# Seven weight conversions instead of four ahead of the joint slots, without blank matmuls, and maxima ahead of reciprocals

## The chip, the core and the metric

The kernel runs on one core of one Trainium2 chip. The metric is the device time of one execution in microseconds (us). A core has five engines that work side by side, each through its own queue in order: TensorE (PE) multiplies and transposes, VectorE (DVE), ScalarE (ACT) and GpSimd (POOL) do elementwise work, and SyncE (SP) issues the DMA transfers.

## What is computed

Sliding-window attention with eight global keys, and behind it two layers with 2048 hidden units. All of it is in float32: the kernel splits operands into a high and a low half and sums three products of them.

```python
def _attn_ref(q, k, v, n_global, n_local):          # 2 x 8 heads x 768 x 64
    scores = scale * np.matmul(q, k.transpose(0, 1, 3, 2))
    keep = is_global | is_local
    dist = np.where(is_global & ~is_local, float(n_local), np.abs(rel).astype(np.float32))
    scores = scores + (-slopes[:, None, None] * dist[None, :, :])[None]
    scores = np.where(keep, scores, -1000000000.0)
    a = np.exp(scores - np.max(scores, axis=-1, keepdims=True))
    a = a / (np.sum(a, axis=-1, keepdims=True) + 1e-09)
    return np.matmul(a, v).astype(np.float32)

def _moe_ref(x, w_in, w_out, alpha):                # 1536 x 512, 512 x 2048, 2048 x 512
    h = x @ w_in
    return ((np.maximum(h, 0.0) + alpha * np.minimum(h, 0.0)) @ w_out).astype(np.float32)

def _moe2_ref(x, w_in, w_out, a, b):                # as above, with g = P(h) / Q(h)
    ...
```

The weights arrive as float64. A weight is turned into float32 by integer operations, which is what is called a conversion here.

## The kernel before

**Steps and slots.** Attention runs in 24 steps (u = 0 to 23), each with two pairs of heads of one block of 128 queries. The steps 0 to 9 run by themselves (`alone`, the opening). The steps 10 to 23 run together with the first layer: `joint_slot(s)`, s = 0 to 15, holds the step 10 + s, the first product of weight chunk s (`first`, 12 matmuls into bank 3) and the second product of the chunk before (`second`, 12 matmuls). From slot 16 on (`plain_slot`) there are only the layers.

**A step.** Scores (PE, L433, three products for each head), maxima (DVE, L448, which also adds the mask and the distances), exponentials and their sums (ACT, L455), sum plus a small number (POOL, L472), reciprocal (DVE, L473), normalising (POOL, L467, four instructions), transposes of the result (PE, L484 and L486) and their copies (ACT, L495), product with the values (PE, L508 and L510) and the split of the result x into halves (ACT L520, DVE L521). The inputs k and q of a later block are transposed (PE, L401) and split (ACT L408 and L411 for the high half, DVE L409 and L412 for the low half, klo and qlo). A step of the opening works on several blocks at different stages: the transposes belong to the step two before, the values to the step three before. The first blocks of k and q come through `boot`, which lies in two of the four stage buffers.

**Conversions.** A weight chunk of 128 x 512 is loaded into one of four stage buffers (SP, L269). ACT scales its upper words (L325). DVE joins them with the lower words (the joins: L314, L315, L316). Then the high half is written, by POOL in the opening (L304) and by ACT in the slots (L302), and DVE subtracts it (L305). These parts are spread over `tick`s: two in a step or slot, one on either side of the other work. A conversion that starts at one tick is joined at the next, or in the tick after when `spread` is set, gets its high half after that and its low half in the following tick. `plan_weights` holds the table of ticks: tick 2u - 20 is the first of step u, 2s the later one of slot s. Before, four conversions start at the ticks -10, -8, -6 and -5 (steps 5 to 7), and from tick 0 to 13 one starts at every tick, two in a slot; then one in a slot. The first half of the weights is also written back to memory (`spill`) and read again later (`reload`).

**Order.** There is no scheduler: each engine's queue is in the order of the code. In `alone` it is scores, sum and reciprocal and normalising of the step before (`both_ready(u - 1)`), maxima of this step (`biased(u)`), low halves of the inputs, values, transfers, exponentials with the first tick between them, transposes and copies, the next inputs, second tick. DVE meets the reciprocal ahead of the maxima there. In the joint slots (`opening`, `turning`) the order is the same.

**The start.** Nine matmuls on the identity (`WARM`), masks (`window_masks`; POOL scales them for each head, L355 and L359), and in the steps 0 and 1 four more matmuls each whose result is not read, the blank matmuls (L578). `global_keys` copies the eight global keys into each of five blocks, high and low: ten small copies on POOL (L416), in step 0 and again in step 12.

Of the kernel before, what the change touches and what calls it, by code (L numbers as in the profile page):

```python
# [8 lines left out]
F32 = mybir.dt.float32  # L9
# [8 lines left out]
P = 128  # L18
B, H, S, D = 2, 8, 768, 64
NB = S // P  # L20
# [4 lines left out]
NC = DM // P  # L25
# [4 lines left out]
NG = 8  # L30
WIN = NPREV + NG + P
KST = P + NG
# [4 lines left out]
NU = NZ // 2  # L37
JOIN = 20
KL, QL, VL, BL = 12, 10, 4, 3
WARM, KEEP = 9, 2  # L40
WL = (4, 6, 8, 10)
LATE = 16
NEARLY = 4
NST = 4
CH = NF // 2
KEPT = CH + 4
# [14 lines left out]
class Kernel:  # L61
# [67 lines left out]
    def constants(self):  # L129
# [7 lines left out]
            )  # L137
        self.boot = {}
        for i in range(2):
            t = self.stage[i].rearrange("p c f w -> p (c f w)").bitcast(F32)  # L140
            for n, nm in enumerate(("k", "q")):
                self.boot[nm, i] = t[:, n * DM : (n + 1) * DM].rearrange("p (h d) -> p h d", h=H)
        for i, heads in ((0, slice(0, H // 2)), (0, slice(H // 2, H)), (1, slice(0, H))):
# [77 lines left out]
    def plan_weights(self):  # L221
        self.steps = [(0, 0, fc, fc % NEARLY) for fc in range(CH)]
        self.steps += [(0, 1, fc, fc % NEARLY) for fc in (*range(NEARLY, CH), *range(NEARLY))]
        self.steps += [(0, 2, fc, fc) for fc in range(NF)]
        self.steps += [(0, g, fc, fc) for g in (0, 1) for fc in range(CH, NF)]
        self.steps += [(1, g, j, j) for g in (2, 0) for j in range(CH)]
        self.steps += [(1, 1, j, j) for j in range(NF)]
        self.steps += [(1, g, j, j) for g in (2, 0) for j in range(CH, NF)]
        runs = [s[:2] for s in self.steps]
        self.begins = {n for n in range(len(runs)) if n == 0 or runs[n - 1] != runs[n]}  # L230
        self.ends = {n - 1 for n in self.begins if n} | {len(runs) - 1}
        self.saves = {n for n in self.ends if runs[n] in runs[n + 1 :]}
        self.adds = {n for n in self.ends - self.saves if runs[n] in SAVED}
        jobs = {}
        for fc in range(CH):
            jobs[2 * fc - 5 if fc > 2 else 2 * fc - 10] = 0, fc, "in", fc % NEARLY
            jobs[2 * fc - 2 if fc else -5] = 0, fc, "out", fc % NEARLY
        half, layer = NGR * CH, NGR * NF
        spare = [(fc, kind) for fc in range(CH, NF) for kind in ("in", "out")]
        for t, (fc, kind) in enumerate(spare):  # L240
            jobs[11 + 2 * t if fc < KEPT else 15 + 2 * t] = 0, fc, kind, None if fc < KEPT else fc
# [6 lines left out]
        times += range(107, 160, 5)  # L248
        for t in times:
            ready = [x for x in todo if x[1] <= t]  # L250
            if ready:
                j, _, kind = job = min(ready)
                todo.remove(job)
                jobs[t] = 1, j, kind, j
        assert not todo
        self.starts = set(jobs)
        self.plan = [jobs[t] for t in sorted(jobs)]
# [67 lines left out]
            nc.scalar.mul(self.de[n % 2], self.staged(n)[:, :, :, 1].bitcast(F32), 2.0**-112)  # L325


    def window_masks(self, pool):
# [14 lines left out]
        nc.vector.tensor_scalar(glo, self.idx, ng, None, ALU.is_lt)  # L343
        nc.vector.tensor_add(dist, rel, far)
        nc.vector.tensor_copy(dist0, dist[:, own])
        nc.vector.scalar_tensor_tensor(only, dist[:, o8], FAR, glo, ALU.is_ge, ALU.mult)
        nc.vector.tensor_scalar(far[:, 0:NG], only, -1.0, 1.0, ALU.mult, ALU.add)
        nc.vector.tensor_mul(dist0[:, 0:NG], dist0[:, 0:NG], far[:, 0:NG])
# [14 lines left out]
    def attention_window(self, pool, moe):  # L363
# [47 lines left out]
            nc.scalar.mul(hi, t, -0.125)  # L411
            return lambda: nc.vector.scalar_tensor_tensor(lo, t, -0.125, hi.bitcast(F32), ALU.mult, ALU.subtract)  # L412

        def global_keys(b):
            for t in (khi, klo) if b < NB - 1 else ():
                nc.gpsimd.tensor_copy(t[:, :, b * KST + P : (b + 1) * KST], t[:, :, 0:NG].bitcast(F32))  # L416

        def width(z):
            return P if (z // 4) % NB == 0 else WIN
# [102 lines left out]
            return lambda: None  # L522

        def inputs(u):
            if u == 0:
                return [("k", 0, far), ("q", 0, far)]
            some = [("k", 1, slice(0, NC)), ("q", 1, slice(0, NC))] if u == 1 else []
# [18 lines left out]

        def keys_of_all(u):
            if u % (2 * NB) == 0 and u < NU:
                for b in range(NB - 1):
                    global_keys(b)  # L550

        transpose_in("k", 0, 4, near)
        transpose_in("q", 0, 5, near)
        bm0, bm1, first_masks, later_masks = self.window_masks(pool)
        first_masks(range(0, H))
        split_in("k", 0, 4, near)()
        split_in("q", 0, 5, near)()
        load_va(0)
        load("k", 2)
        load("q", 2)  # L560
        load_va(1)

        lows = []

        def low_halves():
            while lows:
                lows.pop(0)()

        def alone(u):
            t = 2 * u - JOIN  # L570
            scores(u)
            both_ready(u - 1)
            biased(u)
            low_halves()
            if u < 2:
                later_masks(range(4 * u, 4 * u + 4))
                for _ in range(2 * KEEP):
                    nc.tensor.matmul(banks[2][:, 0:P], ident, ident, start=True, stop=True)  # L578
            values(u - 3)
            fetches(u)  # L580
            exponentials(2 * u)
            low = store_x(u - 3)
            self.tick(False, t in self.starts, spread=True)
            exponentials(2 * u + 1)
            low()
            self.join_step(3)
            transpose_p(u - 2, 6)
            copy_p(u - 2, 6)
            for n, (nm, i, cs) in enumerate(inputs(u)):
                bank = (3, 2)[n % 2]  # L590
                transpose_in(nm, i, bank, cs)
                lows.append(split_in(nm, i, bank, cs))
                if u < 2:
                    low_halves()
            keys_of_all(u)
# [133 lines left out]
    def moe(self):  # L729
# [123 lines left out]
        def joint_slot(s, halves):  # L853
            u = JOIN // 2 + s
            opening, turning = halves or (lambda u: None, lambda u: ())
            if s >= CH + 2 and s < CH + 2 + NEARLY:
                self.reload(s - CH - 2)
            if s == LATE - 1:
                self.spill()
            opening(u)  # L860
            if s:
                self.tick(True, 2 * s - 1 in self.starts)
# [8 lines left out]
                second(s - 1)  # L871
            if s == LATE - 1:
                self.tick(True, 2 * s + 1 in self.starts)

        def plain_slot(s):
            early, late = s - 1, s - 2
# [113 lines left out]
```

## Time and profile before

| | us |
|---|---|
| median of 3 runs (652.05 to 653.6) | 652.1 |
| the profiled execution | 652.37 |
| its span, first to last instruction | 650.6 |
| PE busy | 619.0 |
| DVE busy | 535.2 |
| ACT busy | 377.4 |
| POOL busy | 126.1 |

Busy time is a sum over stages with different limits, so it is read by stretches. The granted clock is the share of its full speed (2.4 GHz) at which TensorE ran: 0.50 is its lower level of 1.2 GHz. A row of the timeline gives start, duration, engine, line, operation, output and inputs, how many instructions stand in the row, and in brackets the idle time of the engine ahead of it with what ended it. In the opening the steps begin on DVE with L448; a joint slot begins on PE with its `first`, L743.

### The profile page before, as it was taken

Reading aid. Unit: us, or ns where it says so; the run is one execution under the profiler, and the core shown is the slowest. Engines: PE = TensorE matmul, PEld = TensorE weight load, DVE = VectorE, ACT = ScalarE, POOL = GpSimd, SP = SyncE. Lnnn points to the kernel's source line nnn. Section 1 sums busy time; section 2 is a strip of 40 time slices with the busy share of each in tenths; the row PEclk is TensorE's granted clock in tenths of the full one; section 3 lists DMA queues with packets and bytes.
Section 4 is the critical chain, followed back from the end, with each engine's and each line's share of the span. In section 5 each row is a group of like instructions: output and inputs, shape, how many; then the busy total and the mean of one; then the engine's idle time right before and its main releaser. Section 6 shows DMA issues by size and latency. Waiting matters only on the chain. (4 is left out here: it accounts for less than half of the span.)

```text
span 650.6 us, 9534 instructions
## 1 busy us (share of the span) xinstructions
PE 619.0 (95%) x3250; PEld 507.8 (78%) x3250; DVE 535.2 (82%) x1015; ACT 377.4 (58%) x787; POOL 126.1 (19%) x220
## 2 busy tenths in 40 slices
PE   7877999899999999999999999999999999999995
PEld 6656777778878888888888878888788888888783
DVE  4587799987756977967979989999999977786985
ACT  2895757666644323323333367687787766766671
POOL 4553311221220000000000003222222222222221
PEclk7998999999999999999999999999999999999999
DMA  8889599978887943421612500121120000300301
GB/s 160 191 224 255 144 286 251 291 235 249 249 277 268 360 144 98 130 65 36 193 62 65 169 26 2 42 94 58 33 97 2 0 1 1 129 2 0 130 0 71
DMA packets 84858, 82.80 MB, mean 127 GB/s; under 512 B 45313, under 2 KB 61953, under 8 KB 84801
## 3 DMA queue, kind: packets, MB, share of 16 engines
q1 hardware_dynamic: 84656, 81.98, 42.1%
q8 instruction: 27, 0.44, 0.3%
q14 instruction: 31, 0.25, 0.1%
q10 hardware_dynamic: 144, 0.13, 0.1%
HBM read 60.21 MB, written 19.92 MB: 123 GB/s over the span
## 5 line engine op out<-in xcount | busy, mean ns | idle before, releaser
L794 POOL TENSOR_TENSOR glo<-act,ghi 128x512 fp32r<-128x512 f32 (+1 forms) x49 | 65.7, 1341 | 385.4 <-ACT ghi L790 372.6
L751 ACT CAST ghi<-bank 128x512 fp32r<-128x512 f32 x48 | 28.2, 588 | 110.6 <-DVE bank L750 93.0
L743 PE MATMUL bank<-xhi,winhi_f 128*128 128x512 f32 x256 | 68.4, 389 | 0.0
L743 PE MATMUL bank<-xhi,winlo_f 128*128 128x512 f32 x256 | 68.4, 389 | 0.0
L743 PE MATMUL bank<-xlo,winhi_f 128*128 128x512 f32 x256 | 68.4, 389 | 0.0
L455 ACT ACTIVATE prob<-prob,stat 128x232 f32<-128x232 f32 (+1 forms) x96 | 44.7, 469 | 26.2 <-DVE stat L448 24.5
L467 POOL TENSOR_SCALAR prob<-prob,rec 128x232 f32<-128x232 f32 (+1 forms) x96 | 41.4, 450 | 93.3 <-DVE rec L473 73.3
L743 PEld LDWEIGHTS bank<-xhi,winlo_f 128*128 128x128 f32 x256 | 48.1, 188 | 10.0
L743 PEld LDWEIGHTS bank<-xhi,winhi_f 128*128 128x128 f32 x256 | 48.0, 188 | 10.0
L743 PEld LDWEIGHTS bank<-xlo,winhi_f 128*128 128x128 f32 x256 | 48.0, 188 | 10.0
L315 DVE SCALAR_TENSOR_TENSOR dx<-de,dx 128x512 int32<-128x512 int32 x64 | 48.2, 754 | 2.2
L752 DVE TENSOR_TENSOR glo<-bank,ghi 128x512 fp32r<-128x512 f32 x48 | 33.1, 689 | 16.8 <-ACT ghi L751 9.4
L790 ACT CAST ghi<-act 128x512 fp32r<-128x512 f32 (+1 forms) x49 | 30.2, 616 | 28.3 <-DVE act L787 28.2
L316 DVE SCALAR_TENSOR_TENSOR dx<-stage,dx 128x512 int32<-128x512 int32 x64 | 44.3, 692 | 2.2
L761 ACT ACTIVATE stage<-bank 128x512 f32<-128x512 f32 (+1 forms) x49 | 28.8, 588 | 29.6 <-PE bank L743 29.6
L749 DVE TENSOR_SCALAR act<-bank,al 128x512 f32<-128x512 f32 x48 | 35.8, 745 | 12.1 <-PE bank L743 12.1
L770 DVE SCALAR_TENSOR_TENSOR stage<-stage,abs_b 128x512 f32<-128x512 f32 (+1 forms) x49 | 36.0, 737 | 11.6 <-ACT stage L762 11.5
L325 ACT ACTIVATE de<-stage 128x512 f32<-128x512 f32 x64 | 42.8, 674 | 0.6 <-DMA stage<-in_moe_w_out_dram 0.6
L809 PE MATMUL bank<-wouthi_f,glo 128*128 128x512 f32 x144 | 41.3, 391 | 0.7 <-POOL glo L794 0.7
L809 PE MATMUL bank<-wouthi_f,ghi 128*128 128x512 f32 x144 | 41.1, 390 | 0.2 <-ACT ghi L790 0.2
L809 PE MATMUL bank<-woutlo_f,ghi 128*128 128x512 f32 x144 | 40.9, 389 | 0.0
L785 DVE SCALAR_TENSOR_TENSOR stage<-stage,cq,bank 128x512 f32<-128x512 f32 (+1 forms) x49 | 35.9, 734 | 3.7 <-ACT bank L775 3.7
(206 smaller groups left out, 1448.8 us busy)
## 6 DMA issues: line engine op xcount, KB each, us to landing
stage<-in_moe_w_in_dram SPq DMA_DIRECT2D x32, 512.0 KB, 4.2
stage<-in_moe_w_out_dram SPq DMA_DIRECT2D x32, 512.0 KB, 4.2
part<-saved_f SPq DMA_DIRECT2D x16, 256.0 KB, 4.3
va<-in_v_dram SPq DMA_DIRECT2D x13, 256.0 KB, 6.2
saved_f<-part SPq DMA_DIRECT2D x12, 256.0 KB, 2.6
out_dram<-part SPq DMA_DIRECT2D x11, 256.0 KB
rawk<-in_k_dram SPq DMA_DIRECT2D x10, 256.0 KB, 5.1
rawq<-in_q_dram SPq DMA_DIRECT2D x10, 256.0 KB
```

The lines of the kernel that those rows point to most:

```text
L315: lambda: nc.vector.scalar_tensor_tensor(y, e, -(2**31), y, ALU.bitwise_and, ALU.bitwise_or),
L316: lambda: nc.vector.scalar_tensor_tensor(y, low, 29, y, ALU.logical_shift_right, ALU.bitwise_or),
L325: nc.scalar.mul(self.de[n % 2], self.staged(n)[:, :, :, 1].bitcast(F32), 2.0**-112)
L455: nc.scalar.activation(p[:, j - e, :w], p[:, j - e, :w], AF.Exp, bias=st[:, j : j + 1], scale=-1.0, accum_out=st[:, 4 + j : 5 + j],)
L467: nc.gpsimd.tensor_scalar(p[:, j, :w], p[:, j, :w], r[:, e + j : e + j + 1], 1.0, ALU.mult, ALU.mult)
L743: nc.tensor.matmul(bk, w["in", a][:, c, :], x[:, c, :], start=e == 0, stop=e == len(seq) - 1)
L749: nc.vector.tensor_scalar(t, h, 0.0, self.al[:, fc : fc + 1], ALU.min, ALU.mult)
L752: return lambda: nc.vector.tensor_sub(lo, h, hi.bitcast(F32))
L770: nc.vector.scalar_tensor_tensor(w, w, self.ab[:, 0:1], ab, ALU.add, ALU.mult)
L785: nc.vector.scalar_tensor_tensor(w, w, self.cq[:, 0:1], r, ALU.add, ALU.mult)
L794: nc.gpsimd.tensor_tensor(lo, u, hi.bitcast(F32), ALU.subtract)
L809: nc.tensor.matmul(y[d], lhs, rhs, start=begin and e == 0, stop=last and e == 2)
```

## The change

It has six parts. (1) In the table of ticks seven conversions start in the opening, at -14, -12, -10, -8, -6, -4 and -2, one in each of the steps 3 to 9; the others start at 0, 2, 3, 5, 6, 8, 9, 11, 12, 13, 14 and then one in a slot, so that to tick 14 there are four in three slots. The loads begin one step earlier (`WL`), and `boot` lies in the stage buffers 2 and 3. (2) The blank matmuls of the steps 0 and 1 are gone. (3) In `alone` the maxima stand ahead of `both_ready`. (4) The far half of the first k and q is transposed and split at the very start, the second block in step 0, each into a bank of its own, and the low halves of the near half go between the masks' instructions. (5) The key copies are two instructions for all five blocks, and stand behind the low halves. (6) Small moves: the constants of the layers one step later, the last spill behind a tick, and the last five conversions of the second layer at 121, 125, 137, 141 and 145 in place of 122, 127, 132, 137 and 142.

```diff
-WARM, KEEP = 9, 2
-WL = (4, 6, 8, 10)
+WARM = 9
+WL = (2, 4, 6, 8)
...
-            t = self.stage[i].rearrange("p c f w -> p (c f w)").bitcast(F32)
+            t = self.stage[NST - 2 + i].rearrange("p c f w -> p (c f w)").bitcast(F32)
...
-        for fc in range(CH):
-            jobs[2 * fc - 5 if fc > 2 else 2 * fc - 10] = 0, fc, "in", fc % NEARLY
-            jobs[2 * fc - 2 if fc else -5] = 0, fc, "out", fc % NEARLY
+        begin = {"in": (-14, -12, -8, -4, 0, 3, 6, 9), "out": (-10, -6, -2, 2, 5, 8, 11, 13)}
...
-        def global_keys(b):
-            for t in (khi, klo) if b < NB - 1 else ():
-                nc.gpsimd.tensor_copy(t[:, :, b * KST + P : (b + 1) * KST], t[:, :, 0:NG].bitcast(F32))
+        def global_keys():
+            for t in (khi, klo):
+                blocks = t.rearrange("p c (b k) -> p c b k", k=KST)[:, :, 0 : NB - 1, P:]
+                first = t[:, :, 0:NG].bitcast(F32).unsqueeze(2).broadcast_to([P, NC, NB - 1, NG])
+                nc.gpsimd.tensor_copy(blocks, first)
...
         transpose_in("k", 0, 4, near)
         transpose_in("q", 0, 5, near)
-        bm0, bm1, first_masks, later_masks = self.window_masks(pool)
+        transpose_in("k", 0, 3, far)
+        transpose_in("q", 0, 2, far)
+        firsts = [split_in("k", 0, 4, near), split_in("q", 0, 5, near)]
+        lows = [split_in("k", 0, 3, far), split_in("q", 0, 2, far)]
...
+        bm0, bm1, first_masks, later_masks = self.window_masks(pool, near_lows)
...
             scores(u)
+            biased(u)
             both_ready(u - 1)
-            biased(u)
             low_halves()
+            keys_of_all(u)
             if u < 2:
                 later_masks(range(4 * u, 4 * u + 4))
-                for _ in range(2 * KEEP):
-                    nc.tensor.matmul(banks[2][:, 0:P], ident, ident, start=True, stop=True)
...
-                bank = (3, 2)[n % 2]
+                bank = 3 if u else 6 + n
...
-            if u == 1:
+            if u == 2:
                 self.moe_constants()
```

**Three places in the order of instructions.** Names: bank is a PSUM bank, stage a stage buffer, dx a joined weight, winlo and woutlo a low half of a weight, rec the reciprocals, prob the scores and probabilities, stat their maxima and sums. The maxima are printed as ISA.

DVE, a whole step of the opening with a conversion, before (the first conversion, in step 6):

```order
L448 ISA prob_255,stat_260<-bank_87,bm_285 128x232
L448 ISA stat_260 128x1
L409 TENSOR_TENSOR klo<-bank_85,khi 128x4x128
L314 TENSOR_SCALAR dx_96<-de_94 128x512
L315 SCALAR_TENSOR_TENSOR dx_96<-de_94,dx_96 128x512
L316 SCALAR_TENSOR_TENSOR dx_96<-stage_90,dx_96 128x512
L521 TENSOR_TENSOR xlo_108<-bank_84,xhi_105 128x2x128
L305 TENSOR_TENSOR winlo__112<-dx_96,winhi__111 128x512
L473 RECIPROCAL rec_263<-rec_263 128x4
L448 ISA prob_256,stat_261<-bank_82,bm_285 128x232
```

and after, in step 5:

```order
L453 ISA prob_259,stat_262<-bank_87,bm_293 128x232
L453 ISA stat_262 128x1
L478 RECIPROCAL rec_263<-rec_263 128x4
L414 SCALAR_TENSOR_TENSOR qlo_253<-bank_85,qhi_251 128x512
L315 TENSOR_SCALAR dx_97<-de_95 128x512
L316 SCALAR_TENSOR_TENSOR dx_97<-de_95,dx_97 128x512
L317 SCALAR_TENSOR_TENSOR dx_97<-stage_91,dx_97 128x512
L526 TENSOR_TENSOR xlo_108<-bank_84,xhi_105 128x2x128
L306 TENSOR_TENSOR winlo__116<-dx_97,winhi__115 128x512
L453 ISA prob_254,stat_260<-bank_82,bm_293 128x232
```

The reciprocal, for which POOL's normalising waits, moved from ahead of the four maxima to behind them, next to the joins.

PE, the end of the scores of step 0 and what follows, before:

```order
L433 MATMUL bank_87<-khi,qlo_252 128x128
L578 MATMUL bank_84<-part_78 128x128 x4
L401 MATMUL bank_85<-part_78,stage_90 128x128 x2
L401 MATMUL bank_84<-part_78,stage_90 128x128 x2
L433 MATMUL bank_82<-khi,qhi_250 128x128
```

and after:

```order
L438 MATMUL bank_86<-khi,qlo_252 128x128
L438 MATMUL bank_87<-khi,qlo_252 128x128
L403 MATMUL bank_88<-part_78,stage_93 128x128 x4
L403 MATMUL bank_89<-part_78,stage_93 128x128 x4
L438 MATMUL bank_82<-khi,qhi_250 128x128
```

The four blank matmuls and the far half of the first block stood there; now it is the second block, in two other banks.

DVE in the joint slot 5, from the low half of x to the low half of the layer's input, before:

```order
L521 TENSOR_TENSOR xlo_109<-bank_84,xhi_106 128x2x128
L305 TENSOR_TENSOR woutlo__118<-dx_96,wouthi__117 128x512
L314 TENSOR_SCALAR dx_98<-de_94 128x512
L315 SCALAR_TENSOR_TENSOR dx_98<-de_94,dx_98 128x512
L316 SCALAR_TENSOR_TENSOR dx_98<-stage_92,dx_98 128x512
L305 TENSOR_TENSOR winlo__124<-dx_97,winhi__123 128x512
L314 TENSOR_SCALAR dx_96<-de_95 128x512
L315 SCALAR_TENSOR_TENSOR dx_96<-de_95,dx_96 128x512
L316 SCALAR_TENSOR_TENSOR dx_96<-stage_93,dx_96 128x512
L749 TENSOR_SCALAR act_99<-bank_85,al 128x512
L750 SCALAR_TENSOR_TENSOR bank_85<-bank_85,act_99 128x512
L412 SCALAR_TENSOR_TENSOR qlo_253<-bank_84,qhi_251 128x512
```

and after:

```order
L526 TENSOR_TENSOR xlo_109<-bank_84,xhi_106 128x2x128
L306 TENSOR_TENSOR woutlo__118<-dx_96,wouthi__117 128x512
L306 TENSOR_TENSOR winlo__124<-dx_97,winhi__123 128x512
L315 TENSOR_SCALAR dx_98<-de_94 128x512
L316 SCALAR_TENSOR_TENSOR dx_98<-de_94,dx_98 128x512
L317 SCALAR_TENSOR_TENSOR dx_98<-stage_92,dx_98 128x512
L752 TENSOR_SCALAR act_99<-bank_85,al 128x512
L753 SCALAR_TENSOR_TENSOR bank_85<-bank_85,act_99 128x512
L414 SCALAR_TENSOR_TENSOR qlo_253<-bank_84,qhi_251 128x512
```

One set of three joins left the slot.

## Rows read from the trace of the kernel before

**Rows 1.** Stages: stretch in us, length, busy time by engine, clock, DMA

```profile
9.10:19.30 10.20, 9.29 (x50) 8.51 (x50) 3.58 (x22) 4.57 (x19) 8.02 (x31) 0.50 1.06 189
19.30:56.90 37.60, 27.29 (x286) 21.09 (x284) 29.77 (x105) 30.44 (x99) 19.28 (x47) 1.00 0.91 232
56.90:60.30 3.40, 3.40 (x30) 2.93 (x28) 2.21 (x12) 2.70 (x9) 1.95 (x5) 0.50 1.13 351
60.30:140.00 79.70, 73.56 (x525) 59.79 (x524) 68.59 (x172) 52.56 (x142) 17.73 (x51) 1.00 0.81 237
```

**Rows 2.** Waits of PE (total, times, longest): 70 to 130, 130 to 141, 400 to 500

```profile
PE bank L508 <- DVE qlo L412: 2.5, 3, 1.5
PE bank L508 <- DVE klo L409: 2.0, 2, 1.0
...
PE bank L508 <- DVE klo L409: 0.8, 1, 0.8
...
PE bank L809 <- POOL glo L794: 0.7, 1, 0.7
```

**Rows 3.** Timeline of PE, first matmuls of the slots 0, 4, 5, 9, 10

```profile
60.66 1.21 PE L743 MATMUL bank<-xhi,winhi__111 128*128 128x512 f32 x4 [0.20 <-DVE klo L409]
...
96.74 1.19 PE L743 MATMUL bank<-xhi,winhi__111 128*128 128x512 f32 x4
...
106.50 1.20 PE L743 MATMUL bank<-xhi,winhi__115 128*128 128x512 f32 x4
...
144.94 1.20 PE L743 MATMUL bank<-xhi,winhi__115 128*128 128x512 f32 x4
...
153.84 1.20 PE L743 MATMUL bank<-xhi,winhi__119 128*128 128x512 f32 x4
```

**Rows 4.** Timeline of DVE, the first joins of two conversions in one slot

```profile
99.44 0.42 DVE L314 TENSOR_SCALAR dx<-de 128x512 int32<-128x512 int32 x1
...
101.83 0.42 DVE L314 TENSOR_SCALAR dx<-de 128x512 int32<-128x512 int32 x1
```

**Rows 5.** Timeline of DVE in the opening: steps 4, 6, 7 and 10

```profile
28.34 0.40 DVE L448 CUSTOM_DVE_ANT_0 prob<-bank,bm 128x232 f32<-128x232 f32 x1
...
35.98 0.40 DVE L448 CUSTOM_DVE_ANT_0 prob<-bank,bm 128x232 f32<-128x232 f32 x1
...
37.86 0.42 DVE L314 TENSOR_SCALAR dx<-de 128x512 int32<-128x512 int32 x1
...
39.65 0.42 DVE L521 TENSOR_TENSOR xlo<-bank,xhi 128x256 fp32r<-128x256 f32 x1
...
41.34 0.37 DVE L448 CUSTOM_DVE_ANT_0 prob<-bank,bm 128x232 f32<-128x232 f32 x1
...
58.63 0.40 DVE L448 CUSTOM_DVE_ANT_0 prob<-bank,bm 128x232 f32<-128x232 f32 x1 [0.96 <-PE bank L433]
```

**Rows 6.** Timeline of the steps 0 and 1: blank matmuls, first reciprocal

```profile
10.91 2.07 PE L578 MATMUL bank<-part 128*128 128x128 f32 x8
...
15.82 2.07 PE L578 MATMUL bank<-part 128*128 128x128 f32 x8
...
16.06 0.18 DVE L473 RECIPROCAL rec<-rec 128x4 f32<-128x4 f32 x1 [1.34 <-POOL rec L472]
```

**Rows 7.** Timeline of POOL and DVE, operations of both at one time

```profile
41.60 1.76 POOL L467 TENSOR_SCALAR prob<-prob,rec 128x232 f32<-128x232 f32 x4 [0.38 <-DVE rec L473]
...
43.20 0.44 DVE L314 TENSOR_SCALAR dx<-de 128x512 int32<-128x512 int32 x1
...
406.24 1.36 POOL L794 TENSOR_TENSOR glo<-act,ghi 128x512 fp32r<-128x512 f32 x1 [3.18 <-issue]
...
406.49 1.67 DVE L315 SCALAR_TENSOR_TENSOR dx<-de,dx 128x512 int32<-128x512 int32 x1
```

**Rows 8.** Timeline of PE, the transposes ahead of the scores of step 10

```profile
56.37 0.67 PE L401 MATMUL bank<-part,rawk 128*128 128x128 f32 x4 [3.35 <-DVE qlo L412]
```

**Rows 9.** Timeline of SP, the transfer of four constants

```profile
16.96 2.81 SPq L186 DMA_DIRECT2D co<-in_moe_a_dram  x1
```

More of the change, by code (lines that the diff above doesn't have):

```diff
@@ L234, in plan_weights @@
         jobs = {}
-        for fc in range(CH):
-            jobs[2 * fc - 5 if fc > 2 else 2 * fc - 10] = 0, fc, "in", fc % NEARLY
-            jobs[2 * fc - 2 if fc else -5] = 0, fc, "out", fc % NEARLY
+        begin = {"in": (-14, -12, -8, -4, 0, 3, 6, 9), "out": (-10, -6, -2, 2, 5, 8, 11, 13)}
+        for kind, times in begin.items():
+            for fc, t in enumerate(times):
+                jobs[t] = 0, fc, kind, fc % NEARLY
         half, layer = NGR * CH, NGR * NF
@@ L240, in plan_weights @@
         for t, (fc, kind) in enumerate(spare):
-            jobs[11 + 2 * t if fc < KEPT else 15 + 2 * t] = 0, fc, kind, None if fc < KEPT else fc
+            jobs[12 + 2 * t if fc < KEPT else 15 + 2 * t] = 0, fc, kind, None if fc < KEPT else fc
         todo = []
@@ L247, in plan_weights @@
         times = [t for t in range(48, 96) if (t % 2 == 0 or t in (55, 71) or t > 82) and t not in (64, 66, 80, 82, 85, 88, 91, 94, 95)]
-        times += range(107, 160, 5)
+        times += (107, 112, 117, 121, 125, *range(137, 160, 4))
         for t in times:
@@ L325, in tick, with window_masks @@
             nc.scalar.mul(self.de[n % 2], self.staged(n)[:, :, :, 1].bitcast(F32), 2.0**-112)
-    def window_masks(self, pool):
+    def window_masks(self, pool, between):
         nc, rel = self.nc, self.rel
@@ L345, in window_masks @@
         nc.vector.tensor_copy(dist0, dist[:, own])
+        between()
         nc.vector.scalar_tensor_tensor(only, dist[:, o8], FAR, glo, ALU.is_ge, ALU.mult)
@@ L524, in inputs @@
         def inputs(u):
-            if u == 0:
-                return [("k", 0, far), ("q", 0, far)]
-            some = [("k", 1, slice(0, NC)), ("q", 1, slice(0, NC))] if u == 1 else []
+            some = [("k", 1, slice(0, NC)), ("q", 1, slice(0, NC))] if u == 0 else []
             i, odd = divmod(u + 3, 2)
@@ L548, in keys_of_all, with near_lows @@
             if u % (2 * NB) == 0 and u < NU:
-                for b in range(NB - 1):
-                    global_keys(b)
+                global_keys()
         transpose_in("k", 0, 4, near)
         transpose_in("q", 0, 5, near)
-        bm0, bm1, first_masks, later_masks = self.window_masks(pool)
+        transpose_in("k", 0, 3, far)
+        transpose_in("q", 0, 2, far)
+        firsts = [split_in("k", 0, 4, near), split_in("q", 0, 5, near)]
+        lows = [split_in("k", 0, 3, far), split_in("q", 0, 2, far)]
+        def near_lows():
+            for low in firsts:
+                low()
+        bm0, bm1, first_masks, later_masks = self.window_masks(pool, near_lows)
         first_masks(range(0, H))
-        split_in("k", 0, 4, near)()
-        split_in("q", 0, 5, near)()
         load_va(0)
@@ L561, in attention_window @@
         load_va(1)
-        lows = []
         def low_halves():
@@ L589, in alone @@
             for n, (nm, i, cs) in enumerate(inputs(u)):
-                bank = (3, 2)[n % 2]
+                bank = 3 if u else 6 + n
                 transpose_in(nm, i, bank, cs)
                 lows.append(split_in(nm, i, bank, cs))
-                if u < 2:
-                    low_halves()
-            keys_of_all(u)
             self.tick(False, t + 1 in self.starts, spread=u < JOIN // 2 - 1)
-            if u == 1:
+            if u == 2:
                 self.moe_constants()
@@ L857, in joint_slot @@
                 self.reload(s - CH - 2)
-            if s == LATE - 1:
-                self.spill()
             opening(u)
@@ L873, in joint_slot @@
                 self.tick(True, 2 * s + 1 in self.starts)
+                self.spill()
         def plain_slot(s):
```

## The prediction

> **What bounds the kernel now.** I read three views in this order: the stages with granted clock, then what TensorE (PE) waits for, then the two engines that it waits for. The stages [rows 1] show three different limits. From 60 to 140 us, the joint slots, PE is busy 73.6 of 79.7 us and VectorE (DVE) 68.6, and the granted clock is 1.00. Every wait of PE in that stretch ends with DVE writing a low half, qlo or klo [rows 2]: 2.5 + 2.0 + 0.8 = 5.3 us. From 19 to 57 us, the later opening, nothing is packed: PE is busy 27.3 of 37.6 us, DVE 29.8, ScalarE (ACT) 30.4. Before 19 us and again from 56.9 to 60.3 us the clock stood at 0.50, its 1.2 GHz level. After 140 us PE hardly waits; the one late wait that this change can touch is 0.7 us [rows 2].
>
> So a conversion in a joint slot is dear only where DVE has no room. The first pass of slot 4 began at 96.74 and that of slot 5 at 106.50 [rows 3]: 9.76 us with two conversions, of which PE waited 1 to 1.5. Slots 9 to 10, with one conversion, took 8.90 (144.94 to 153.84), with no wait: that is PE's own work. One conversion costs DVE 101.83 - 99.44 = 2.39 us [rows 4]. So DVE needs about 9.76 us with two, 7.4 with one, and 8.2 on average at four in three slots.
>
> **Part by part. The joint slots, -5.2.** Three conversions leave these slots. DVE's average of 8.2 lies under PE's 8.9. A slot that still has two runs 0.86 over, one with one leaves 1.5, and before the change PE's first wait of about 1 us came only after three full slots in a row. The change has two such slots in a row at most (6 and 7). I take back 5.2 of the 5.3 us; the ends are 4.0 and 5.6.
>
> **The first steps, -4.3 up to step 4.** Two groups of blank matmuls go, 2.07 us each [rows 6], both ahead of transposes that the next scores need: at most 4.1. DVE waited 1.34 us for the sums of POOL at step 1 [rows 6], behind ten small key copies that become two: at most 1.3 more. Against it stand the transposes of the far half, now ahead of the first scores, and low halves ahead of the masks, together some tenths. The maxima no longer wait for the reciprocals, but the mask rows on POOL then become the last to arrive. The ends are -3.7 and -5.2; I take -4.3, so the maxima of step 4 begin at 24.0 in place of 28.34 [rows 5].
>
> **Steps 4 to 9, +6.0.** Before, from the maxima of step 4 to those of step 10 it is 58.63 - 28.34 = 30.3 us [rows 5]. Only step 6 on had joins. Such a step took 41.34 - 35.98 = 5.36 us [rows 5]: four maxima, low half of the input, three joins from 37.86, x's low half at 39.65, then a short wait for POOL's high half and the low half of the weight. DVE works in all of it but that wait, so it sets the length. Now each of the steps 4 to 9 has a conversion, and step 9 the joins of a second one (39.65 - 37.86 = 1.8).
>
> The length of a step changes too. The reciprocal now stands behind the maxima, so POOL's four normalisings (1.76 us [rows 7]) start 1.3 us later and run beside the three joins in place of beside the maxima. The trace shows what two such operations do to each other: the join of 406.49 took 1.67 us in place of 0.69, because a POOL subtraction ran from 406.24 to 407.60 [rows 7]; the join waited it out. A normalising is short and lets go early: the join of 43.20 began while the last of the four was running and took 0.44 in place of 0.42 [rows 7]. With a hold of about 0.3 us for each, three of them fall between the joins: the second join waits about 0.15 us, the third 0.1, and POOL's high half comes some 0.15 later. I take 5.75 us a step. The ends are 5.36 (no meeting) and 6.65 (single file: maxima 1.3, 0.35 until POOL starts, 1.76, 1.8, and some 1.45 for the two halves, of the 1.69 from 39.65 to 41.34). The Trainium skill, SBUF — State Buffer, section "Who interferes with whom", says that VectorE and GpSimd share a port pair as an exclusive lock, held for the whole instruction, when VectorE has two SBUF inputs or a two-port mode; that is the third rival below, and row 406.49 agrees with it.
>
> So step 10 begins at 24.0 + 5 x 5.75 + 5.75 + 1.8 = 60.3 in place of 58.63. The two parts together give -4.3 + 6.0 = **+1.7**.
>
> **The hand-over, +2.3.** The first pass of the joint slots waits for bank 3, which DVE frees 2.0 us after the maxima of step 10 begin (58.63 to 60.66 [rows 3, 5]). Before, PE idled 3.35 us at 53 to 56.4 [rows 8], then ran 3.4 us at clock 0.50 [rows 1]: work that lay ahead of the slots, half of it hidden by DVE. Now DVE's double step 9 leaves PE idle for some 4.5 us right ahead of the first pass, so the low clock falls on dense slots. One stretch of 3.4 us at half speed costs 1.7, two cost 3.4, none 0; I take 2.3. The Trainium skill, TensorE: Matmul & The Clock Gate, section "What's actually happening", has the throttled state as the default, released by activity, and so speaks against taking blank matmuls out. The trace bears it out only in part: with the blanks in place the clock was 0.50 for 10.2 us [rows 1].
>
> **The rest.** The last weights are converted at other ticks, two of them one or two ticks earlier and three later, away from the end of a group near 470 us, where PE waited 0.7 us for POOL's low half: -0.5, between 0 and -0.7. The constants' three transfers move one step later and now stand ahead of the second weight load on SP; the issue of one of them held SP for 2.81 us [rows 9], so ACT may wait as long for that load in step 4. DVE's longer steps 4 and 5 cover it; without that cover it costs up to 2.8. The weights use other stage buffers than the first keys and queries, so no load waits for them. The last spill moves behind a tick and delays the reloads by some 3 us; they are read 20 us later. The keys' copies in slot 2 shrink beside idle time of POOL: nothing.
>
> **Sum.** -5.2 + 1.7 + 2.3 - 0.5 = -1.7. The profiled execution took 652.37 us (650.6 of span and 1.8 around it), which gives 650.7; the median of the runs, 652.1, lies 0.3 lower. I forecast **650.4**: within 0.3% of before, which is about what a measurement of this kernel can tell from no change (650.1 to 654.1).
>
> **The rivals.**
> *Joins and normalisings do not hurt each other, and the clock holds.* For it: the 0.44 of row 43.20. Step 10 then begins at 24.0 + 5 x 5.36 + 7.16 = 58.0, which is -0.7; with the clock at half its price, +1.2, the sum is -0.7 + 1.2 - 5.2 - 0.5 = -5.2, or **647.0**.
> *A step of the opening runs in single file.* At 6.65 us a step, six steps cost 5.4 more than I took: **655.8**, slower than before. It decides from about 6.4 us a step. For it: row 406.49, where a join waited a whole POOL operation. Against it: row 43.20.
> *The joint gain does not come.* If slots with two conversions still make PE wait, 5 us less are won: **655**. Against it: slots 8 to 10 with one conversion show no wait.
> *It does not do what it says:* seven conversions do begin before the slots by the order of instructions, so I give this nothing.
>
> **How the numbers follow.** Forecast, 650 to 654: 0.44. First rival, below 650.1: 0.40. Single file: 0.12. No joint gain: 0.04. Faster 0.40, within 0.44, slower 0.16. For eight in ten the range leaves out the far ends of the first and the second rival: 646.8 to 654.8. Both signs stay in it; the forecast's own range is 649 to 653.
>
> **What would show it.** Right: no wait of PE on qlo or klo over 0.5 us from 60 to 140 us; maxima of step 4 at 23 to 25 us; steps 4 to 8 of 5.6 to 6.0 us on DVE, with joins over 0.75 us; the first pass at 61.5 to 63 us, at clock 0.50. Wrong: steps of 5.4 or 6.5 us, a first pass before 60 us, or joint slots still over 9.3 us.

## The result, and the profile after

The changed kernel took 657.16 us, median of four runs (655.97 to 657.87), against 652.09 for the kernel before beside it: a ratio of 1.0069, interval 1.0054 to 1.0083. It is slower, and the time lies outside the forecast range. The profiled execution took 655.97 with a span of 654.1 (before: 652.37 and 650.6). It is the shortest of its four runs, so the traces can explain 3.5 of the 5.1 us between the medians; where the other 1.6 arise, no trace here shows. A ratio, here and below, compares the runs of both kernels and need not be the quotient of their medians. Differences between two variants are differences of their medians, whose runs spread by 0.3 to 3 us; one of about 1 us says little by itself, and the marks of the traces carry the readings.

Seven marks of the two timelines show where it went. Each is the start of a row: the first maximum of a step on DVE, or the first matmul of a slot's `first` on PE.

| mark | before | after | difference |
|---|---|---|---|
| maxima of step 4 | 28.34 | 24.38 | -3.96 |
| maxima of step 10 | 58.63 | 66.33 | +7.70 |
| first pass of slot 0 | 60.66 | 68.32 | +7.66 |
| first pass of slot 1 | 69.49 | 79.61 | +10.12 |
| first pass of slot 16 | 200.91 | 205.74 | +4.83 |
| last first pass | 628.45 | 634.42 | +5.97 |
| end of the span | 650.6 | 654.1 | +3.5 |

So the first steps gain 4, steps 4 to 9 lose 11.7, slot 0 loses 2.5, the joint slots gain 5.3, the stretch to the last first pass loses 1.1, and the tail is 2.5 shorter.

The large term is in one step. DVE's timeline (start, duration, engine, line, operation; in brackets the idle time ahead and what ended it) has the maxima of steps 4, 5, 6 and 10, and between two of them one join:

```profile
24.38 0.40 DVE L453 CUSTOM_DVE_ANT_0 prob<-bank,bm 128x232 f32<-128x232 f32 x1 [0.80 <-PE bank L438]
...
30.03 0.39 DVE L453 CUSTOM_DVE_ANT_0 prob<-bank,bm 128x232 f32<-128x232 f32 x1
...
39.85 0.69 DVE L317 SCALAR_TENSOR_TENSOR dx<-stage,dx 128x512 int32<-128x512 int32 x1 [5.20 <-DMA stage<-in_moe_w_in_dram]
...
41.89 0.39 DVE L453 CUSTOM_DVE_ANT_0 prob<-bank,bm 128x232 f32<-128x232 f32 x1
...
66.33 0.37 DVE L453 CUSTOM_DVE_ANT_0 prob<-bank,bm 128x232 f32<-128x232 f32 x1
```

Step 4 takes 5.65 us, step 5 takes 11.86, and steps 6 to 8 take 5.64 each. In step 5 the third join of a weight waits 5.2 us for a weight load. Yet ScalarE had scaled that same weight at 29.55, so its load had landed by then. The ScalarE row and, from SP's timeline, the load that it waited for and a later one:

```profile
29.55 0.67 ACT L326 ACTIVATE de<-stage 128x512 f32<-128x512 f32 x1 [2.69 <-DMA stage<-in_moe_w_in_dram]
...
25.26 0.43 SPq L270 DMA_DIRECT2D stage<-in_moe_w_in_dram  x1
...
33.48 0.38 SPq L270 DMA_DIRECT2D stage<-in_moe_w_in_dram  x1
```

The join waited for the load issued at 33.48, 6.4 us earlier, and not for the one at 25.26. The stages (columns as in [rows 1]) show the stall, the hand-over at low clock, and the joint slots, where PE no longer waits:

```profile
30.00:42.00 12.00, 6.04 (x50) 5.32 (x52) 5.29 (x17) 6.75 (x21) 3.24 (x7) 0.76 1.11 308
...
60.00:68.30 8.30, 3.44 (x32) 2.71 (x32) 7.55 (x23) 5.08 (x17) 5.79 (x10) 0.71 0.97 290
68.30:79.60 11.30, 10.86 (x76) 8.86 (x76) 4.37 (x14) 5.76 (x16) 1.35 (x5) 0.76 0.55 152
79.60:140.00 60.40, 60.34 (x426) 49.30 (x424) 52.26 (x131) 39.00 (x109) 13.18 (x35) 1.00 0.75 211
```

### The profile page after: what moved, and what is told of

Same layout as the page of the kernel before. It is cut to its first block, busy times and chain, and to the rows that moved or that the text cites. A ratio compares the mean times of both kernels' runs of the same rounds, so it can differ in the third digit from the quotient of the medians.

```text
span 654.1 us, 9467 instructions
## 1 busy us (share of the span) xinstructions
PE 623.7 (95%) x3234; PEld 510.6 (78%) x3234; DVE 538.4 (82%) x1015; ACT 376.2 (58%) x785; POOL 133.6 (20%) x206
## 4 chain that ended last, share of the span: by engine, by line
PE 79%; DVE 10%; POOL 4%; ACT 3%; issue 2%; DMA 1%; SPq 0%; DVEq 0%; POOLq 0%; ACTq 0%
PE bank L812 36%; PE bank L746 36%; POOL prob L472 2%; PE bank L513 2%; PE bank L438 2%; DVE prob L453 1%; DVE dx L316 1%; PE bank L489 1%; DMA dwinhi_f<-spare 1%; PE bank L515 1%; DVE act L790 1%; PE bank L491 1%; DVE stage L789 1%; PE bank L403 1%; DVE stage L788 1%
## 5 line engine op out<-in xcount | busy, mean ns | idle before, releaser
L797 POOL TENSOR_TENSOR glo<-act,ghi 128x512 fp32r<-128x512 f32 (+1 forms) x49 | 67.2, 1371 | 385.3 <-ACT ghi L793 364.0
L472 POOL TENSOR_SCALAR prob<-prob,rec 128x232 f32<-128x232 f32 (+1 forms) x96 | 46.7, 504 | 95.6 <-DVE rec L478 60.1
L316 DVE SCALAR_TENSOR_TENSOR dx<-de,dx 128x512 int32<-128x512 int32 x64 | 50.9, 795 | 2.2
L317 DVE SCALAR_TENSOR_TENSOR dx<-stage,dx 128x512 int32<-128x512 int32 x64 | 45.9, 718 | 7.3 <-DMA stage<-in_moe_w_in_dram 5.2
```

What stands on the lines that cost most here:

```text
L316: lambda: nc.vector.scalar_tensor_tensor(y, e, -(2**31), y, ALU.bitwise_and, ALU.bitwise_or),
L317: lambda: nc.vector.scalar_tensor_tensor(y, low, 29, y, ALU.logical_shift_right, ALU.bitwise_or),
L472: nc.gpsimd.tensor_scalar(p[:, j, :w], p[:, j, :w], r[:, e + j : e + j + 1], 1.0, ALU.mult, ALU.mult)
L797: nc.gpsimd.tensor_tensor(lo, u, hi.bitcast(F32), ALU.subtract)
```

## Which load the join waits for

The table `WL` issues one weight load at the end of each of the steps 1 to 4 (2, 4, 6, 8 are twice the step; loads and weights are counted from 0 here). The first conversion now begins in step 3, and its joins run in step 4, ahead of the table's last entry. Behind the joins stands `load_more`, which refills the ring of four stages: it issues loads 3 and 4. Then the table's fourth entry calls `load_next`, which takes whatever comes next: load 5, into the stage of weight 1, whose low words DVE has not read yet. The order of SP's instructions shows this load with what it waits for, first in the changed kernel, then with the table stopped at four loads (`waits` names the queues and engines that it waits for):

```
L270 DMA stage_91<-in_moe_w_in_dram 128x4x256 [waits DMAHW2_49,Activation_49]
...
L270 DMA stage_91<-in_moe_w_in_dram 128x4x256 [waits DMAHW3_49,DVE_49,Activation_49]
```

In the changed kernel it waits for ScalarE's scaling but not for DVE's join; the join, later in program order, waits for the load. It also takes the last three bits of the numbers of the second `w_in` chunk from the fourth chunk, which load 5 brings, so this is a change of what is computed as well. (The expectation below calls it another matrix; it is another chunk of the same one.) Before, `WL` began one step later, but the first joins only came in step 6, when all four loads had been issued.

**Four loads only.**

```diff
-            if 2 * u in WL:
+            if 2 * u in WL and self.loads < NST:
```

> The changed kernel with one condition added: the opening's own table of weight loads stops once four loads have been issued. Theory A: in the changed kernel the first conversion's joins now come in step 4, ahead of the table's fourth entry; the join's own refill then issues loads 3 and 4, and the table's entry issues load 5 into the stage that still holds weight 1, so that the third join of step 5 has to wait for load 5 (5.2 us at 39.85) and takes its low words from that other matrix. With the condition, step 5 has no wait for a load over 0.7 us and lasts 5.65 us like its neighbours, the maxima of step 10 begin near 60.1 in place of 66.33, and the time falls by 6.2 from 657.2 to 651.0 (649.5 to 652). Rival C: the wait is for a late load behind the constants' transfers; then the condition changes nothing and the time stays at 656 to 658.

Measured: 650.84 (ratio to before 0.9956, 0.9933 to 0.9979). Theory A holds. The wait for a load is gone; step 5 lasts 7.17 in place of 11.86, step 10 begins at 62.32. Load 5 now goes out when the join that reads its stage is done:

```profile
35.30 0.69 DVE L317 SCALAR_TENSOR_TENSOR dx<-stage,dx 128x512 int32<-128x512 int32 x1
...
36.05 0.37 SPq L270 DMA_DIRECT2D stage<-in_moe_w_in_dram  x1
```

The medians are 6.3 us apart, the spans of the two traces 4.4. Step 5 does not last the 5.65 that I expected: 1.5 us are left, of which below.

**Constants out of the way, the overrun left in.**

```diff
-            if u == 2:
+            if u == 5:
                 self.moe_constants()
```

> The changed kernel with the three transfers of the constants issued at the end of step 5 in place of step 2, so that they no longer stand ahead of the second weight load. Theory A (a load into a stage that is still read): the wait of the third join in step 5 stays at 4 to 6 us and the time at 656 to 658; the wait of 2.69 us of ScalarE for the second load in step 4 shrinks below 1 us and gives nothing back. Rival C (the constants make the second load late, and that is what the join waits for): the wait of the join goes and the time falls by about 5, to 652.

Measured: 654.02 (1.0012, 0.9997 to 1.0028). The join still waits for a load, as A says:

```profile
38.09 0.69 DVE L317 SCALAR_TENSOR_TENSOR dx<-stage,dx 128x512 int32<-128x512 int32 x1 [4.22 <-DMA stage<-in_moe_w_in_dram]
```

ScalarE's wait of 2.69 is gone. But the time fell by 3.1 where I expected no change. The traces show 1.8 of it: load 5 lands earlier too (join at 38.09 in place of 39.85, step 10 at 64.56 in place of 66.33). C names a second, smaller cost and not the cause of the stall.

## The constants ahead of the second weight load

With four loads only, ScalarE waits 2.96 us in step 4 for the second load; the forecast took this as covered by DVE. DVE loses nothing by it in step 4, but in step 5 it waits 0.91 for ScalarE's high half and 0.46 for the scores, with PE at clock 0.53, and the step lasts 7.17. The wait of ScalarE, the two waits of DVE, and the stage of step 5:

```profile
30.14 0.68 ACT L326 ACTIVATE de<-stage 128x512 f32<-128x512 f32 x1 [2.96 <-DMA stage<-in_moe_w_in_dram]
...
33.23 0.69 DVE L414 SCALAR_TENSOR_TENSOR qlo<-bank,qhi 128x512 fp32r<-128x512 f32 x1 [0.91 <-ACT qhi L413]
...
37.88 0.40 DVE L453 CUSTOM_DVE_ANT_0 prob<-bank,bm 128x232 f32<-128x232 f32 x1 [0.46 <-PE bank L438]
...
30.70:37.90 7.20, 5.62 (x39) 4.96 (x40) 5.29 (x17) 6.77 (x21) 3.27 (x7) 0.53 1.13 294
```

ScalarE, with its wait behind it, is busy for 6.77 of these 7.2 us.

> The changed kernel with four opening loads only, and the constants' three transfers at the end of step 5 in place of step 2. Against four opening loads alone (650.84). Theory: with the constants ahead of it the second weight load reached ScalarE 2.96 us late in step 4, the chain behind that made step 5 last 7.17 in place of 5.64, so that term of the prediction was not covered; now ScalarE waits under 0.5 us for that load, step 5 lasts 5.6 to 5.8, and the time falls by 1.5 to about 649.3. Rival (step 5 was long only because the clock stood at 0.53 there): the step stays above 6.8 us and the time does not change.

The edit is that of the constants above, on top of the four loads. Measured: 651.76 (0.998, 0.9969 to 0.9991), no gain. Step 5 did fall to 5.64, but step 7 rose to 6.75: the constants' first reader on ScalarE, left at the end of step 6, now waited for them, and behind it POOL's sums and DVE's reciprocal.

```profile
44.78 0.20 ACT L192 ACTIVATE abs_b<-co 128x2 f32<-128x2 f32 x1 [3.36 <-DMA co<-in_moe_b_dram]
...
44.67 0.18 DVE L478 RECIPROCAL rec<-rec 128x4 f32<-128x4 f32 x1 [1.02 <-POOL rec L477]
```

So I moved the readers too.

```diff
-            if u == 2:
+            if u == 5:
                 self.moe_constants()
-            if u == 6:
+            if u == 9:
                 self.moe_constants_ready()
```

> The changed kernel with four opening loads only, the constants' transfers at the end of step 5 and their first readers at the end of step 9 in place of step 6. In the run before, with the readers left at step 6, ScalarE waited 3.4 us for the constants there and step 7 lasted 6.75. Against four opening loads alone (650.84). Theory: both waits of ScalarE are gone, all steps from 4 to 8 last 5.6 to 5.7, step 10 begins at 60.7 to 61.1 in place of 62.3, and the time falls by 1.3 to 1.6, to about 649.4. Rival (the long step 5 was the clock's doing, which differs between runs): the time stays at 650.5 to 651.8.

Measured: 650.85 (0.9964, 0.9952 to 0.9977). All steps from 4 to 8 last 5.65 and step 10 begins at 60.99, 1.33 earlier than with four loads alone, as the theory says. But the median did not move. In the traces the first pass of slot 0 comes 1.33 earlier, slot 0 takes 11.37 in place of 10.64, at a lower clock, and at the end of the span 0.4 is left, less than the runs of one kernel differ. The stage of slot 0 in both, first with four loads only, then with the constants moved:

```profile
64.30:75.00 10.70, 10.27 (x77) 8.48 (x77) 4.37 (x14) 5.81 (x16) 1.39 (x5) 0.81 0.59 170
```

```profile
63.00:74.40 11.40, 10.98 (x77) 8.97 (x77) 4.34 (x14) 5.78 (x16) 1.37 (x5) 0.76 0.72 221
```

The late load is thus a real 1.5 us in step 5. The low clock of that step went with it (1.00 in step 5 once the constants had moved), but it seems the smaller part: with blanks ahead of slot 0 (below) ScalarE's wait was 2.99, the clock of step 5 0.76 in place of 0.53, and the step still lasted 7.02. Whether the 1.5 reaches the end depends, as far as these traces go, on the hand-over behind it. The last pair below has it again.

## Maxima ahead of reciprocals

On top of the four loads, `both_ready(u - 1)` again stands ahead of `biased(u)`.

> The changed kernel with the condition on the loads, and with the reciprocals ahead of the maxima again in the opening. Theory: the joins no longer run beside POOL's normalisings, so the joins of 0.83 us return to 0.69 and steps 6 to 9 last 5.36 in place of 5.64; the first steps lose some 1 to 1.5 because the maxima wait for the sums again. Against the kernel with the condition alone: -1.7 + 1.2 = -0.5 (-1.7 to +1). Rival: the length of a step is set by something else, the joins are no cause; then steps stay at 5.6 and the time rises by 1 or more.

Measured: 650.13 (0.9944, 0.9922 to 0.9967). Both halves of the theory show: step 4 begins at 26.71 in place of 25.07, and every step from 4 to 8 lasts 5.36 in place of 5.64, step 5 in place of 7.17. That step gains 1.5 more than its neighbours because step 4 begins later, so that ScalarE waits only 0.89 for the second load. Of the 1.8 us by which step 10 begins earlier (60.50), the order itself thus gives only 0.3. Joins and normalisings of one step, with maxima first (four loads only):

```profile
45.15 2.79 POOL L472 TENSOR_SCALAR prob<-prob,rec 128x232 f32<-128x232 f32 x4 [1.49 <-DVE rec L478]
...
45.92 0.83 DVE L316 SCALAR_TENSOR_TENSOR dx<-de,dx 128x512 int32<-128x512 int32 x1
46.78 0.83 DVE L317 SCALAR_TENSOR_TENSOR dx<-stage,dx 128x512 int32<-128x512 int32 x1
48.56 0.69 DVE L306 TENSOR_TENSOR winlo__120<-dx,winhi__119 128x512 fp32r<-128x512 f32 x1 [0.61 <-POOL winhi__119 L305]
```

and with reciprocals first:

```profile
43.06 1.76 POOL L472 TENSOR_SCALAR prob<-prob,rec 128x232 f32<-128x232 f32 x4 [0.38 <-DVE rec L478]
...
45.13 0.69 DVE L316 SCALAR_TENSOR_TENSOR dx<-de,dx 128x512 int32<-128x512 int32 x1
45.86 0.69 DVE L317 SCALAR_TENSOR_TENSOR dx<-stage,dx 128x512 int32<-128x512 int32 x1
47.29 0.69 DVE L306 TENSOR_TENSOR winlo__120<-dx,winhi__119 128x512 fp32r<-128x512 f32 x1 [0.41 <-POOL winhi__119 L305]
```

Two joins lengthen by 0.14 each, the four normalisings from 1.76 to 2.79. The Trainium skill, SBUF — State Buffer, section "Who interferes with whom", has a VectorE instruction with two SBUF inputs contend with a GpSimd instruction that reads SBUF. The trace agrees that they contend; but a join lost only 0.14 us, no whole normalising of 0.44.

**The same part alone, on the kernel before.** In the kernel before, the two lines in `alone` change places.

> The kernel before with one part of the change alone: maxima ahead of reciprocals in the opening. Theory (joins beside POOL's normalisings cost 0.28 us a step): the four steps with joins last 5.64 in place of 5.36, +1.1; the first steps no longer wait for POOL's sums, up to -1.3; together between -0.2 and +1.0. Of the end of the program: in the trace of the kernel before 7.2 us lie between the last store's issue and the end, in all changed kernels 4.65 to 5.0. If that belongs to the one execution profiled, the end here is 4.6 to 5.0 too; if it belongs to the kernel before, it is 7.

Measured: 651.11 (0.9987, 0.9975 to 0.9999), 1.7 under the median of before (652.78) where I expected -0.2 to +1.0; the ten runs lie between 650.67 and 653.37, and the interval all but touches 1. The first steps gained more than I thought, 2.58 by step 4, and step 10 began 2.82 earlier. The join steps were uneven: 6.16, 5.64 and a double one of 7.01 (before 5.36, 5.37, 7.67). Of 2.85 us at slot 0, 1.6 were given back at once, since slot 0 took 10.42 in place of 8.83, part of it at low clock:

```profile
57.80:68.30 10.50, 10.07 (x77) 8.35 (x77) 4.50 (x14) 5.46 (x15) 1.40 (x5) 0.83 0.37 85
```

From the last store's issue to the end it was 6.7 us, nearer to the 7.2 of before than to the 4.65 to 5.1 of the changed kernels. So the shorter tail, 2.5 us of the sum, goes with the changed kernel. It lies wholly behind the last stores: from the last first pass to the last store's issue on SP it is 14.6 us before and after. Why the end is shorter, no run here shows.

## The blank matmuls of steps 0 and 1

The edit puts the four blank matmuls behind `later_masks` in each of the steps 0 and 1 back, on top of the four loads.

> The changed kernel with the condition on the loads, and with the blank matmuls of steps 0 and 1 put back. Theory of the prediction: each of the two groups delays the scores behind it by up to 2.07 us, so the maxima of step 4 begin 2 to 4 us after 24.4 and the time rises by 2 to 4 against the kernel with the condition alone. Rival (the blanks pay by holding up the clock): the granted clock is 1.00 for longer before 50 us, the steps that PE sets get shorter, and the time falls by up to 1.5 or stays.

Measured: 652.39 (0.9989, 0.9974 to 1.0005), 1.5 over four loads alone, less than the 2 to 4 that I expected. Step 4 began at 27.52, 2.45 later, as expected; but step 5 then lasted 5.64, since ScalarE waited only 0.65 for the second load, and step 10 began 0.94 later. The clock was no better: 0.50 from 9 to 21 us with the blanks in place, and 0.77 at the hand-over (63 to 76 us). Taking the blanks out was right.

## The late ticks

```diff
-        times += (107, 112, 117, 121, 125, *range(137, 160, 4))
+        times += range(107, 160, 5)
```

> The changed kernel with four opening loads only, and with the last eleven conversions at the ticks of the kernel before (107, 112, 117 and so on by fives). Against four opening loads alone (650.84). Theory: the new ticks cost, the difference to the kernel before grows by 0.8 us between 455 and 485 us of the trace and by 0.3 near 522; with the old ticks both go and the time falls by 1.1 to about 649.8. Rival of the prediction (the new ticks gain 0.5): the time rises by 0.5 to 651.3.

Measured: 649.77 (0.9958, 0.9944 to 0.9973), 1.07 under four loads alone: the new ticks cost what the traces showed. From the first pass of slot 16 to the last first pass it is 428.64 with four loads only and 427.54 with the old ticks, as before the change (427.54). With the old ticks PE's waits after 210 us are again those of before, 1.2 for ScalarE and 0.7 for POOL, in place of 2.3 for ScalarE; these rows make up 0.4 of the 1.1. One of the two new stalls in PE's timeline (four loads only):

```profile
465.33 1.21 PE L812 MATMUL bank<-wouthi_f,ghi 128*128 128x512 f32 x4 [0.58 <-ACT ghi L793]
```

ScalarE's high half came late because it had waited 1.19 us for DVE, which is the engine that the conversions load.

## The hand-over

**The second joins of step 9 left for slot 0.**

```diff
-            self.tick(False, t + 1 in self.starts, spread=u < JOIN // 2 - 1)
+            self.tick(False, t + 1 in self.starts, spread=True)
```

> The changed kernel with four opening loads only, and with the second conversion's joins of step 9 left for the first joint slot, where VectorE waits 4.63 us for the first pass. Against four opening loads alone (650.84). Theory: the maxima of step 10 and the first pass of slot 0 come 1.8 us earlier (60.5 and 62.5), nothing waits for the joins, and the time falls by 1.8 to about 649.0. Rival: VectorE is then late with the low halves in slot 0 or 1 and the 1.8 us come back there, so that the time stays at 650 to 651.

Measured: 648.82 (0.9941, 0.9924 to 0.9957). Slot 0 began 1.81 earlier (62.50), took 8.81 in place of 10.64 at clock 1.00, and no matmul waited for the joins. The median fell by 2.0, close to the theory's 1.8; the profiled execution is the shortest of the four (647.16, the others 648.8), and its trace gains 3.6 by slot 1.

**Blank matmuls where PE is idle.**

```diff
             if s:
                 self.tick(True, 2 * s - 1 in self.starts)
+            for _ in range(0 if s else 16):
+                nc.tensor.matmul(banks[7][:, 0:P], self.ident, self.ident, start=True, stop=True)
             first(s)
```

> The changed kernel with four opening loads only, and with 16 blank matmuls ahead of the first pass of slot 0, where TensorE waits 3.84 us for klo. Against four opening loads alone (650.84). Theory of the prediction (idle time ahead of the first pass brings the low clock onto it): the granted clock stays at 1.00 through slot 0, from the first pass of slot 0 to that of slot 1 it takes 8.9 us in place of 10.64, and the time falls by 1.7 to about 649.1. Rival: the clock falls all the same, the blanks run at 0.50 and reach past the end of the wait, and the time rises by up to 3.

Measured: 648.9 (0.9943, 0.9926 to 0.996). That is 1.9 under four loads alone. The blanks filled the wait, and slot 0, from 63.53 to 72.32, took 8.79. PE's timeline:

```profile
59.62 3.84 PE L865 MATMUL bank<-part 128*128 128x128 f32 x32
63.53 1.20 PE L746 MATMUL bank<-xhi,winhi__111 128*128 128x512 f32 x4
```

Its stage row has the clock at 1.00:

```profile
63.50:72.30 8.80, 8.35 (x76) 7.08 (x76) 4.39 (x14) 5.75 (x16) 1.36 (x5) 1.00 0.90 267
```

Compare the clock of 0.81 without them. The mechanism of the hand-over term, idle PE ahead of dense slots, is shown.

## A version that beats both

Four loads only, the old late ticks, the joins of step 9 in slot 0, and reciprocals first from step 4 on (maxima first in steps 0 to 3):

```diff
+            if u < 4:
+                biased(u)
             both_ready(u - 1)
+            if u >= 4:
+                biased(u)
```

> The changed kernel with four opening loads only, the late ticks of the kernel before, the second joins of step 9 left for slot 0, and reciprocals ahead of the maxima from step 4 on (maxima first in steps 0 to 3). If the parts add up: 650.84 - 1.1 (late ticks) - 2.0 (joins in slot 0) - 1.5 (steps of 5.36 in place of 5.64 from step 4 on) = 646.2 (645.5 to 647.5). If the gains of the opening overlap: 647.5 to 649.

Measured: 646.73 (0.991, 0.9893 to 0.9926). Step 4 lasted 5.94, the others 5.37 or 5.38. With the constants and their readers moved as well:

> The same combination, with the constants' transfers at the end of step 5 and their readers at the end of step 9. If ScalarE's wait for the second weight load was what made step 5 long: 1.5 less than the combination without this, 644.7 (644 to 646). If the clock was: no difference.

Measured: 644.68 (0.9876, 0.9859 to 0.9892), 8 us under the kernel before. The steps last 5.35 to 5.37, step 10 begins at 57.66, and in this execution the clock stands at 1.00 in all stages up to the tail:

```profile
19.00:57.60 38.60, 28.68 (x292) 22.82 (x292) 31.62 (x103) 31.30 (x97) 21.79 (x48) 1.00 0.99 253
57.60:59.60 2.00, 0.03 (x1) 0.00 (x0) 2.00 (x11) 1.47 (x6) 1.69 (x4) 1.00 0.99 367
59.60:68.50 8.90, 8.43 (x77) 7.10 (x77) 6.12 (x17) 5.93 (x16) 1.70 (x5) 1.00 1.06 289
```

Of the 2.2 between the two spans, 0.77 lie ahead of slot 0 and 1.56 in slot 0, which ran partly at low clock without the constants moved (10.39 against 8.83); the rest differs by 0.1 the other way. This compares one trace of each. Two of the four runs with the constants moved, 645.26 and 645.54, had a mean clock of 0.98 in place of 1.00, so that moving the constants settles the clock of slot 0 is not shown.

## Why the prediction was wrong

**The step that failed** is in the part "The rest", where loads were costed at nothing: "The weights use other stage buffers than the first keys and queries, so no load waits for them". That looked at who had the stages before, and not at the two places that issue loads. `WL` moved by one step and the first joins by two, so the refill overtook the table. Its price was 11.86 - 7.17 = 4.7 us in step 5. The order of the instructions shows it without any time: on SP the sixth weight load does not wait for DVE's join that reads the same stage.

**A second sentence of that part failed too**: "DVE's longer steps 4 and 5 cover it; without that cover it costs up to 2.8". The cover held in step 4 and not in step 5; the cost was 1.5, inside its own bound. I took DVE as the only engine that sets a step; ScalarE's delay came to DVE by way of its high half (0.91) and of the scores (0.46).

**The late ticks** were given -0.5 and cost 1.1: the wait for POOL [rows 2] went, and two for ScalarE came, which the forecast left out.

**Right, point by point.** The joint slots: from slot 1 to slot 16 it was 131.42 and is 126.13, -5.3 for a forecast of -5.2, with no wait of PE from 79.6 to 140 us where [rows 2] had 5.3. That the size fits so well is in part luck: the slots 1 to 7 gained 6.0, more than their waits, 8 and 9 lost 1.1 (PE waited 0.3 there for a weight's low half and 0.2 for qlo), and 13 and 14 gained 0.4; and PE's own work, taken as 8.9 for each slot from slot 9, is 8.0 in slots 3 and 4. The first steps: maxima of step 4 at 24.38 for 24.0. The length of a step: 5.64 for 5.75, with joins of 0.83; neither 5.36 nor 6.65, so the first rival falls, and so does the single file (the second in the list of rivals, which the prediction once calls the third). The time that the single file gave, 655.8, is the nearest to the measured one, but its mechanism did not occur: a right number for a wrong reason. The hand-over: the low clock fell on slot 0 and cost 2.5 for 2.3, though it lasted longer than the one or two stretches of 3.4 us that I allowed. Two signs failed with the loads: step 5 of 11.86 us, and a first pass at 68.32 where 61.5 to 63 was named.

**The sum again**, with what was measured: first steps -4.0; steps 4 to 9 +5.4 without the two load costs, which add 4.7 and 1.5; slot 0 +2.5; joint slots -5.3; late +1.1; tail -2.5, which I had not forecast and which stays open. That is +3.4, and the spans differ by 3.5, against 5.1 for the medians. Without the overrun the kernel takes 650.84, close to the 650.4 forecast, but this is partly luck: the tail of -2.5 hides the errors of the two other terms, +1.5 for the constants and +1.6 for the late ticks.

## What to carry to other kernels

When the start of a pipeline moves, list every place that draws from its ring of buffers, tables and refills alike, and follow in program order that each buffer is last read before it is next loaded; a wait that appears on a reader for a load may be a load into a buffer that it still needs. A transfer that comes late on an engine with room to spare can still cost where that engine's results are awaited a step later. And time won ahead of a dense stage can be lost again to the clock if it turns into idle time of TensorE. Here other work or blank matmuls in that idle time gained 1.9 to 2.0 us, and blank matmuls ahead of work that others awaited cost 1.5.

## What was not expected of the hardware

The clock at the start differed between executions of nearly the same instructions, and it did not matter there. From 0 to 19 us, first the changed kernel, then four loads only, whose first steps are the same:

```profile
0.00:19.00 19.00, 14.48 (x79) 11.88 (x79) 11.07 (x56) 9.30 (x33) 9.22 (x35) 0.73 0.88 170
```

```profile
0.00:19.00 19.00, 15.28 (x78) 12.72 (x78) 10.89 (x56) 9.30 (x31) 8.93 (x34) 1.00 0.89 170
```

The first had half clock from 8.9 to 22.5 us and began step 4 at 24.38, the second had full clock and began it at 25.07. Three more variants with half clock in part of that time began it at 24.40 to 24.58, three with full clock at 25.00 to 25.37; those with half clock had begun step 0 by 0.3 us earlier, and why is open. At the hand-over low clock made slot 0 longer by 1.6 to 2.9 us in the variants, against the 8.8 at full clock. Beside the joins, the normalisings of POOL lost more (2.79 for 1.76 for the four) than the joins themselves.
